# Reordering the front of a fused attention, channel-mix and expert kernel: planner ranks, GpSimd rounding, early weights

## The chip, the cores and the metric

The kernel runs on one core of one Trainium2 chip, in one launch. The metric is the device time of that launch in microseconds (us). Engines are named as in the profile: PE is TensorE, DVE is VectorE, ACT is ScalarE, POOL is GpSimd, SP is SyncE, whose queue issues nearly all DMAs here.

## The reference, cut to what matters

Three stages, each feeding the next: a local and global attention over 4 batches of 8 heads; a channel mix (two mixed inputs, a squared-relu product and a gated product); and a mixture of eight experts, in which every row goes to one expert.

```python
# attention, per batch and head: 512 local rows (window of 32 both ways + 32 global keys), 32 global rows
out_g = sm(scale*q_g @ k_all.T) @ v_all
out_l = sm(concat(scale*q_l @ k_g.T, where(mask, scale*q_l @ k_l.T, -1e9))) @ concat(v_g, v_l)
x = concat(out_g, out_l) per head, heads side by side        # (4, 544, 512)
# channel mix; x_prev is x moved down by one row
xk = mu_k*x + (1-mu_k)*x_prev;  xr = mu_r*x + (1-mu_r)*x_prev
x = sigmoid(xr @ w_r) * (max(xk @ w_k, 0)**2 @ w_v)          # w_k 512x1024, w_r 512x512, w_v 1024x512
# experts: row s goes to e (argmax of x @ w_gate, or the row before's choice)
out[b,s] = p[e] * (max(x @ w1[e], 0) @ w2[e])
```

The inputs w_k, w_r, w_v of the channel mix arrive as 64-bit floats; the kernel reads them as pairs of 32-bit integers.

## The kernel before, in words

**Units.** Attention is cut into 16 units (one batch, two heads); units 0 to 3 make batch 0. A unit is loaded (`load`, L120: q, k and the global rows; `load_v`, L133: ten DMAs for v), transposed into place (`prep`, `prep_g`), and then has two kinds of work. *Items* 0 to 3 are its local rows: `twin` (L178) makes the scores of two items on PE, `item` (L194) does the softmax on DVE (L204), ACT (L208), DVE (L211) and POOL (L214), then PE transposes the weights (L221, tile ptp) and ACT copies them out (tile ph). `gitem` (L284) is item 4, the 32 global rows: scores (L291, tiles sga, sgb), softmax, transposes (L311, tile ptg), copy out (tile ph, by DVE at L114). `values` (L243) multiplies the weights by v: for units 0 to 3 one product for each item as it gets ready (PE tiles av and, for item 4, avg), for units 4 to 15 all five at once. An av product is copied into the channel mix's input xT by ACT (L264). An avg product goes through `turn_g` (L267): ACT scales it (L272, tile og), PE transposes it (L275, tile avt), DVE copies it into xT (L279). A PSUM place "av" of one bank serves av, avg and avt of units 0 to 3, and the place "g" (one) is held from a unit's `gitem` scores until its `turn_g` ends.

**Channel mix.** `weight` (L407) turns one part of w_k (8 parts), w_r (4) or w_v (8) from 64-bit into a rounded 32-bit tile h and a remainder l: a DMA on SP (L417), ACT (L424), three DVE operations (L426, L428, L430), ACT rounds (L432), POOL subtracts (L434). `mix` (L449) makes xk and xr for a group of 256 rows, two of the four 128-row blocks of d_model at a time (blocks 0 and 1 need units 0 and 1, blocks 2 and 3 need units 2 and 3, for batch 0): POOL (L460), DVE (L463), ACT (L465), POOL (L467). PE then multiplies with w_k (tile psk), w_r (psr) and w_v (psv), three products for each (L21, L23, L24). There are nine groups, of which the first lies wholly in batch 0. The experts follow, under an order written out by hand, which the change does not touch.

**What sets the order.** `Sched` (L42) is a planner that runs when the program is built. Each piece of work is a generator of steps; a step names an engine and an assumed duration. At each planned moment, of the steps that are ready it emits the one with the lowest (rank, number in order of addition). SP's DMA issues are an engine ("Q") of the planner too. Ranks: loads -2, w_k parts ahead of the rest PE0=-1.5 (the first N0=3), consts and v loads -1, unit starts and transposes 0, mixes PM=0.5, scores, items, values and `turn_g` 1, other w_k and w_r parts PW=1.5, w_v parts and outputs 2, products of the channel mix 4. The framework beneath may still move an instruction in the emitted order; every engine executes its own list strictly in order.

```python
    for k,i in [("wk",i) for i in range(8)]+...: sched.add(m.weight(k,i),PV if k=="wv" else PE0 if k=="wk" and i<N0 else PW)
```

Of the kernel before, what the change touches and what calls it, by code (L numbers as in the profile page):

```python
# [11 lines left out]
AF=mybir.ActivationFunctionType; ALU=mybir.AluOpType; X=mybir.AxisListType.X  # L12
# [12 lines left out]

N0=3; PE0=-1.5; PC=-1; PW=1.5; PV=2; PM=0.5
NF=4
EV={"kn":"A","qn":"D","g":"D",0:"A",1:"A",2:"A",3:"A"}  # L30
LN=8 ; PL=8
# [8 lines left out]
def op(e,d,need=(),free=(),when=None): return e,d,need,free,when  # L40
def wait(f): return "",0.0,(),(),f
class Sched:  # L42
# [23 lines left out]
    def run(s):  # L66
        while s.L:
            while s.one(): pass
            if not s.L: break
            T=[t for t in [x[3] for x in s.L]+list(s.busy.values())+[t for t,_ in s.left] if t>s.t]  # L70
            assert T, [(x[0],x[2]) for x in s.L]
            s.t=min(T)
            for t,k in s.left:
                if t<=s.t: s.places[k]+=1
            s.left=[y for y in s.left if y[0]>s.t]
# [8 lines left out]
class Attn:  # L84
# [109 lines left out]
    def item(s,sched,u,i,S_,held):  # L194


        nc=s.nc; b,pr=divmod(u,4)
        ks=s.cols(i); w=1 if i in (1,2) else .87
        parts=s.parts(u)
        p=s.pt_.pop(0)  # L200
        mx=s.sb.tile([P,8],F32,tag="mx",name="mx",bufs=5)
        yield op("D",.64*w,(),held)
        for h in range(2):
            i_=nc.vector.tensor_tensor_reduce(out=p[:,h,ks],in0=S_[h],in1=s.mask[:,ks],scale=-0.125,scalar=3e38,op0=ALU.add,op1=ALU.min,accum_out=mx[:,h:h+1])  # L204
        s.free_=[i_.ins.name]
        yield op("A",.2+.93*w)
        for h in range(2):
            nc.scalar.activation(p[:,h,ks],p[:,h,ks],AF.Exp,bias=mx[:,h:h+1],scale=-1.0,accum_out=mx[:,4+h:5+h])  # L208
        nc.scalar.activation(mx[:,4:6],mx[:,4:6],AF.Copy,bias=1e-9)
        yield op("D",.15)  # L210
        nc.vector.reciprocal(mx[:,6:8],mx[:,4:6])  # L211
        yield op("G",.87*w)
        for h in range(2):
            nc.gpsimd.tensor_scalar(out=p[:,h,ks],in0=p[:,h,ks],scalar1=mx[:,6+h:7+h],scalar2=0.0,op0=ALU.mult,op1=ALU.add)  # L214
        yield op("P",.43,("pt","ph"),("p",),when=lambda: u in s.V and s.taken(u))
        s.took[u]+=1
        pt=s.ps.tile([P,2,2,P],F32,tag="pt",name="ptp",bufs=2)
        for c in range(2):

            for h in range(2):  # L220
                nc.tensor.transpose(pt[:,c,h],p[:,h,c*96:c*96+P],s.ident)  # L221
        s.pt_.append(p)
        P_=s.weights()
        yield from s.split(u,EV[i],[P_],pt.rearrange("p c h q -> p c (h q)"),"pt",(.48,.61))
        yield wait(None)
        s.H[u][i]=(P_,s.made)
        if u<NQ: sched.add(s.values(sched,u,(i,),"av"),1)
    def visit(s,after,c=mybir.DependencyClass.NoSync):


# [12 lines left out]
    def values(s,sched,u,which,*place):  # L243


        nc=s.nc; b,pr=divmod(u,4)
        yield op("P",.2+sum(.6 if i==4 else .45 for i in which),place,("ph",)*len(which),when=lambda: u in s.V and all(i in s.H[u] for i in which))
        V=s.V[u]; mm=s.visit([s.H[u][i][-1] for i in which]); rows=[slice(0,HD),slice(HD,P)]
        if 4 in which:
            G,mx=s.H[u][4][:2]  # L250
            og=s.ps.tile([P,512],F32,tag=place[-1],name="avg",bufs=len(place))[:,:HD]
            for c in range(5):
                for h,r in enumerate(rows): mm(og[r],G[:,c*64:(c+1)*64],V[:,min(c,3),c//4,r],start=c==0,stop=c==4)
            sched.add(s.turn_g(u,og,mx,place[-1],len(place)),1)
        s.vdone[u]+=len(which)
        tiles=[i for i in which if i<4]
        if not tiles: return
        o=s.ps.tile([P,512],F32,tag="av",name="av",bufs=1)
        for j,i in enumerate(tiles):
            for c in range(2):  # L260
                for h,r in enumerate(rows): mm(o[r,j*P:(j+1)*P],V[:,i,c,r],s.H[u][i][0][:,c,h*P:(h+1)*P],start=c==0,stop=c==1)
        n=P*len(tiles); c0=1+SG+tiles[0]*P
        yield op("A",.07+.00104*n,(),("av",))
        nc.scalar.activation(s.xT[b][:,pr,c0:c0+n],o[:,:n],AF.Copy)  # L264
        yield wait(None)
        s.odone[u]+=len(tiles)
# [17 lines left out]
    def gitem(s,sched,u):  # L284

        nc=s.nc; b,pr=divmod(u,4); kw,gT=s.T[u]["k"],s.T[u]["g"]
        parts=s.parts(u)
        yield op("P",.75,("s","s","g"))
        a=s.ps.tile([P,512],F32,tag="s",name="sga",bufs=2)[:64]; g=s.ps.tile([P,512],F32,tag="s",name="sgb",bufs=2)[:64,:32]
        for o,k in ((a,kw[:,:,:,32:160]),(g,gT[:,:,64:96])):  # L290
            for m,(x,y_) in enumerate(parts): nc.tensor.matmul(o,gT[:,x,:64],k[:,y_],start=m==0,stop=m==len(parts)-1)  # L291
        s.sdone[u]+=1
        p=s.pg[:64]
        M=s.sb.tile([P,8],F32,tag="mg",name="mxg",bufs=2); mx=M[:64]
        yield op("D",1.1)
        nc.vector.reduce_max(mx[:,0:1],a,axis=X)
        nc.vector.reduce_max(mx[:,1:2],g,axis=X)
        nc.vector.tensor_reduce(out=mx[:,2:3],in_=mx[:,0:2],axis=X,op=ALU.max)
        nc.vector.tensor_scalar(out=mx[:,2:3],in0=mx[:,2:3],scalar1=-0.125,scalar2=None,op0=ALU.mult)
        yield op("A",.92,(),("s","s"))  # L300
        nc.scalar.activation(p[:,32:544],a,AF.Exp,bias=mx[:,2:3],scale=0.125,accum_out=mx[:,4:5])
        s.free_=[nc.scalar.activation(p[:,544:576],g,AF.Exp,bias=mx[:,2:3],scale=0.125,accum_out=mx[:,5:6]).ins.name]
        yield op("D",.28)
        nc.vector.scalar_tensor_tensor(out=mx[:,6:7],in0=mx[:,4:5],scalar=1e-9,in1=mx[:,5:6],op0=ALU.add,op1=ALU.add)
        nc.vector.reciprocal(M[0:32,7:8],mx[0:32,6:7])
        nc.vector.reciprocal(M[96:128,7:8],mx[32:64,6:7])
        yield op("P",.55,("pt","ph"),when=lambda: u in s.V and s.taken(u))
        s.took[u]+=1
        pt=s.ps.tile([P,512],F32,tag="pt",name="ptg",bufs=2)
        for c in range(5):  # L310
            nc.tensor.transpose(pt[:,c*64:c*64+P],s.pg[:,min(c*P,480):min(c*P,480)+P],s.ident)  # L311
        G=s.weights().rearrange("p c q -> p (c q)")[:,:320]
        yield from s.split(u,EV["g"],[G],pt[:,:320],"pt",(.32,.4))
        yield wait(None)
        s.H[u][4]=(G,M,s.made)
        if u<NQ: sched.add(s.values(sched,u,(4,),"av"),1)
    def spare(s,u): return u<4 and u%2==1
    def same(s,u): return [v for v in range(u) if s.spare(v)==s.spare(u)]
    def loads(s,units):
# [3 lines left out]
    def run(s,sched,units,may):  # L323
        for u in units:
            yield wait(lambda: u in s.nat and may(u) and all(s.sdone[v]>=5 for v in s.same(u)))
            s.sdone[u]=s.vdone[u]=s.odone[u]=0; s.H[u]={}; s.took[u]=0
            if s.spare(u): kw,qT,gT=s.kwe,s.qTe,s.gTe
            else:
                dt=F32 if s.early(u) else F32R
                qT=s.sb.tile([P,2,512],dt,tag="qT",name=f"qT{u}",bufs=1); kw=s.sb.tile([P,2,4,224],dt,tag="kw",name=f"kw{u}",bufs=1)  # L330
                gT=s.sb.tile([P,2,96],dt,tag="gT",name=f"gT{u}",bufs=1)
            s.T[u]=dict(k=kw,q=qT,g=gT,n=0,have=False)
            sched.add(s.prep(u,"kn"),0); sched.add(s.prep(u,"qn"),0); sched.add(s.prep_g(u),0)
            yield wait(lambda: s.T[u]["n"]==3)
            for i in (0,2): sched.add(s.twin(sched,u,i),1)
            sched.add(s.gitem(sched,u),1)
            if u>=NQ: sched.add(s.values(sched,u,(4,0,1,2,3),"av","pt"),1)

def band(nc,const):

# [9 lines left out]
class Mix:  # L350
# [56 lines left out]
    def weight(s,k,i):  # L407


        nc=s.nc; place="raw"+"v"*(k=="wv")  # L410
# [11 lines left out]
        h,l=[v(s.W[k+x]) for x in "hl"]  # L422
        m=s.temp("w").rearrange("p (c f) -> p c f",c=c); a=m.bitcast(I32)
# [4 lines left out]
        nc.vector.scalar_tensor_tensor(out=a,in0=hi,scalar=-0x80000000,in1=a,op0=ALU.bitwise_and,op1=ALU.bitwise_or)  # L428
        yield op("D",.6,(),(place,))
        nc.vector.scalar_tensor_tensor(out=a,in0=lo,scalar=29,in1=a,op0=ALU.logical_shift_right,op1=ALU.bitwise_or)  # L430
        yield op("A",.52)
        nc.scalar.activation(h,m,AF.Copy)  # L432
        yield op("G",1.23,(),("r",))
        nc.gpsimd.tensor_sub(l,m,h.bitcast(F32))  # L434
        yield wait(None)
# [284 lines left out]
def phase1(tc,ctx,i,const,y,ident,x,slots,early,place,right):  # L720
# [38 lines left out]
    sched.add(a.run(sched,units,lambda u: u<8 or min(m.mixed)>=(u//4-1)*S),0)  # L759
    for k,i in [("wk",i) for i in range(8)]+[("wr",i) for i in range(4)]+[("wv",i) for i in range(8)]: sched.add(m.weight(k,i),PV if k=="wv" else PE0 if k=="wk" and i<N0 else PW)  # L760
    sched.add(m.mixes(sched,groups),PM)
# [360 lines left out]
```

## Time and profile before

| | |
|---|---|
| median of 3 runs | 742.79 us (742.07 to 744.51) |
| the profiled execution's own time | 741.31 us |
| its span, first to last instruction | 739.6 us |
| PE busy | 682.3 us (92%) |
| DVE, ACT, POOL busy | 444.7, 371.9, 301.4 us |
| mean granted PE clock | 0.961 |

A span is what the profiler's first and last instruction enclose; 1.7 us of the execution lie around it. Rows of a timeline are: start, duration, engine, line, operation, output<-inputs, shape, count; in brackets the idle time of the engine just before it and what ended that. SPq rows are DMA issues on SP's queue. Rows of a table of stretches are: from and to, length, then busy time and count of each engine, the granted PE clock, the DMA share, GB/s. Of a product (L234, L239) the first row stands for all its matmuls.

### The profile page before, as it was taken

The page shows a single profiled execution, that of the slowest core. Times are in us where ns is not written, and L with a number is a line of the kernel's source. Part 1 is how long each engine was busy: PE and PEld are TensorE (multiplying, and loading weights), DVE is VectorE, ACT ScalarE, POOL GpSimd, SP SyncE. Part 2 cuts the span into 40 slices and gives each one's busy share as a digit, 9 for nine tenths or more (in the row PEclk, how much of TensorE's full clock was granted, in tenths as well). Part 3 has the DMA queues.
Part 4 walks back from the last instruction along what each step waited for, and adds up shares of the span by engine and source line. Part 5 has one row for each costly group of instructions (what it writes and reads, how often), then busy time and mean ns, then how long its engine had stood idle before and what let it go on. Part 6 is the DMA issues. An engine that isn't in the chain of part 4 may idle for free. (4 is left out here: it accounts for less than half of the span.)

```text
span 739.6 us, 14192 instructions
## 1 busy us (share of the span) xinstructions
PE 682.3 (92%) x4962; PEld 583.3 (79%) x4962; DVE 444.7 (60%) x1361; ACT 371.9 (50%) x942; POOL 301.4 (41%) x434
## 2 busy tenths in 40 slices
PE   4786969999999999989998999999799999979897
PEld 3564658898888988879987898877689889969785
DVE  6489477857676574774537964778554435324361
ACT  4678576674474663645645432417544325115251
POOL 5457476724443252551423522115725405121431
PEclk9787799999999999999999999999999999999999
DMA  6575154212202211202103200418946607233440
GB/s 156 126 227 167 34 135 136 53 53 55 58 14 58 70 25 52 63 14 70 24 16 131 86 30 15 142 33 292 355 148 188 205 24 235 93 118 129 138 142 22
DMA packets 93184, 76.39 MB, mean 103 GB/s; under 512 B 70350, under 2 KB 74446, under 8 KB 93074
## 3 DMA queue, kind: packets, MB, share of 16 engines
q1 hardware_dynamic: 89618, 64.27, 29.5%
q0 software_dynamic: 3456, 10.75, 4.1%
q8 instruction: 56, 0.92, 0.5%
q14 instruction: 54, 0.44, 0.2%
HBM read 66.08 MB, written 9.44 MB: 102 GB/s over the span
## 5 line engine op out<-in xcount | busy, mean ns | idle before, releaser
L214 POOL TENSOR_SCALAR pl<-pl,mx 128x192 f32<-128x192 f32 (+1 forms) x128 | 64.3, 518 | 97.9 <-DVE mx L211 87.5
L21 PE MATMUL psk<-xs,slot0h 128*128 128x256 f32 x256 | 73.7, 292 | 1.1 <-ACT xs L465 1.1
L24 PE MATMUL psk<-xs,slot0l 128*128 128x256 f32 x256 | 73.4, 287 | 0.0
L23 PE MATMUL psk<-xs,slot0h 128*128 128x256 f32 x256 | 72.9, 285 | 0.0
L208 ACT ACTIVATE pl<-pl,mx 128x192 f32<-128x192 f32 (+1 forms) x128 | 58.6, 460 | 21.4 <-DVE mx L204 17.9
L460 POOL TENSOR_SCALAR xm<-xT,mut 128x256 f32<-128x256 f32 (+6 forms) x96 | 44.5, 479 | 47.4 <-DVE xT L279 15.9
L910 ACT ACTIVATE hh<-ph 128x256 fp32r<-128x256 f32 (+2 forms) x56 | 22.4, 400 | 79.2 <-PE ph L24 52.8
L467 POOL TENSOR_TENSOR xs<-xm,xs 128x512 fp32r<-128x512 f32 (+1 forms) x36 | 45.4, 1272 | 33.1 <-ACT xs L465 33.1
L21 PE MATMUL psv<-slot1h,kh 128*128 128x512 f32 x136 | 54.8, 403 | 0.0
L24 PE MATMUL psv<-slot1h,kl 128*128 128x512 f32 x136 | 54.3, 399 | 0.0
L23 PE MATMUL psv<-slot1l,kh 128*128 128x512 f32 x136 | 54.2, 399 | 0.0
L911 DVE SCALAR_TENSOR_TENSOR hl<-ph,hh 128x256 fp32r<-128x256 f32 (+2 forms) x56 | 24.7, 442 | 47.0 <-ACT hh L910 44.5
L111 ACT ACTIVATE ph<-ptp 128x512 f32<-128x512 f32 x64 | 37.6, 593 | 29.9 <-PE ptp L221 29.8
L21 PEld LDWEIGHTS psk<-xs,slot0h 128*128 128x128 f32 x256 | 48.8, 193 | 1.5 <-ACT xs L465 1.2
L221 PE MATMUL ptp<-ident,pl 128*128 128x128 f32 x256 | 44.8, 301 | 5.3 <-POOL pl L214 4.8
L23 PEld LDWEIGHTS psk<-xs,slot0h 128*128 128x128 f32 x256 | 48.5, 189 | 0.7 <-POOL xs L467 0.2
L24 PEld LDWEIGHTS psk<-xs,slot0l 128*128 128x128 f32 x256 | 48.5, 189 | 0.2
L882 POOL DMA_INDIRECT xs<-y,idx x23 | 26.7, 1163 | 50.5 <-PE pt L889 23.4
L463 DVE SCALAR_TENSOR_TENSOR xm<-xT,mut,xm 128x256 f32<-128x256 f32 (+6 forms) x96 | 39.9, 447 | 7.7 <-POOL xm L460 7.6
L221 PEld LDWEIGHTS ptp<-ident,pl 128*128 128x128 f32 x256 | 32.2, 153 | 13.7 <-POOL pl L214 9.1
L21 PE MATMUL ph<-xh,slot2h 128*128 128x256 f32 (+1 forms) x128 | 37.9, 296 | 2.1 <-issue 2.1
L239 PE MATMUL av<-ph,ve 128*64 128x128 f32 x480 | 37.9, 292 | 0.0
(603 smaller groups left out, 2185.0 us busy)
## 6 DMA issues: line engine op xcount, KB each, us to landing
st<-in_moe_w_dram SPq DMA_DIRECT2D x42, 512.0 KB, 4.2
sw<-in_moe_w_dram SPq DMA_DIRECT2D x22, 512.0 KB, 4.0
y<-r SPq DMA_DIRECT2D x17, 256.0 KB, 2.0
qn<-in_q_l_dram SPq DMA_DIRECT2D x32, 128.0 KB, 2.9
kn<-in_k_l_dram SPq DMA_DIRECT2D x32, 128.0 KB, 2.9
earlyh<-in_moe_w_k_dram SPq DMA_DIRECT2D x8, 512.0 KB, 4.1
raw<-in_moe_w_v_dram SPq DMA_DIRECT2D x8, 512.0 KB, 4.4
ve<-in_v_l_dram SPq DMA_DIRECT2D x32, 96.0 KB, 2.1
```

The source lines that it names most:

```text
L21: i=nc.tensor.matmul(out,wh,xh,start=first,stop=False)
L23: nc.tensor.matmul(out,wh,xl,start=False,stop=False)
L24: return nc.tensor.matmul(out,wl,xh,start=False,stop=last)
L111: s.made=nc.scalar.activation(out[0],x,AF.Copy).ins.name
L208: nc.scalar.activation(p[:,h,ks],p[:,h,ks],AF.Exp,bias=mx[:,h:h+1],scale=-1.0,accum_out=mx[:,4+h:5+h])
L214: nc.gpsimd.tensor_scalar(out=p[:,h,ks],in0=p[:,h,ks],scalar1=mx[:,6+h:7+h],scalar2=0.0,op0=ALU.mult,op1=ALU.add)
L221: nc.tensor.transpose(pt[:,c,h],p[:,h,c*96:c*96+P],s.ident)
L239: with t.high_priority(t.cur_priority-len(first)): i=s.nc.tensor.matmul(*a,**k)
L460: nc.gpsimd.tensor_scalar(out=x[:,u,o:o+k],in0=s.xT[b][:,c,q:q+k],scalar1=m[:,1,c:c+1],scalar2=0.0,op0=ALU.mult,op1=ALU.add)
L463: nc.vector.scalar_tensor_tensor(out=x[:,u,o:o+k],in0=s.xT[b][:,c,1+q:1+q+k],scalar=m[:,0,c:c+1],in1=x[:,u,o:o+k],op0=ALU.mult,op1=ALU.add)
L467: nc.gpsimd.tensor_sub(xl[:,cs,:n],x[:,:,:n],xh[:,cs,:n].bitcast(F32))
L882: s.nc.gpsimd.indirect_dma_start(out=s.xs[i][:,j,:],out_offset=None,in_=s.y,in_offset=IndirectOffsetOnAxis(ap=s.idx[:,ch:ch+1],axis=0))
```

## The change

Three edits, all in the attention and channel-mix stage. N0 goes from 3 to 1: one part of w_k, not three, ranks ahead of unit 0; parts 1 and 2 get PW=1.5 as the others. `values` and `turn_g` are added with rank 0.5 instead of 1. Parts 0 to 3 of w_k are rounded by POOL, not ACT, with a planned 0.6 us.

```diff
-N0=3; PE0=-1.5; PC=-1; PW=1.5; PV=2; PM=0.5
+N0=1; PE0=-1.5; PC=-1; PW=1.5; PV=2; PM=0.5
@@ item
-        if u<NQ: sched.add(s.values(sched,u,(i,),"av"),1)
+        if u<NQ: sched.add(s.values(sched,u,(i,),"av"),0.5)
@@ values
-            sched.add(s.turn_g(u,og,mx,place[-1],len(place)),1)
+            sched.add(s.turn_g(u,og,mx,place[-1],len(place)),0.5)
@@ gitem
-        if u<NQ: sched.add(s.values(sched,u,(4,),"av"),1)
+        if u<NQ: sched.add(s.values(sched,u,(4,),"av"),0.5)
@@ run
-            if u>=NQ: sched.add(s.values(sched,u,(4,0,1,2,3),"av","pt"),1)
+            if u>=NQ: sched.add(s.values(sched,u,(4,0,1,2,3),"av","pt"),0.5)
@@ weight
-        yield op("A",.52)
-        nc.scalar.activation(h,m,AF.Copy)
+        if k=="wk" and i<4:
+            yield op("G",.6)
+            nc.gpsimd.tensor_scalar(out=h,in0=m,scalar1=1.0,scalar2=0.0,op0=ALU.mult,op1=ALU.add)
+        else:
+            yield op("A",.52)
+            nc.scalar.activation(h,m,AF.Copy)
```

## Rows read from the trace of the kernel before

**Rows 1.** The page's busy times.

```profile
PE 682.3 (92%) x4962; PEld 583.3 (79%) x4962; DVE 444.7 (60%) x1361; ACT 371.9 (50%) x942; POOL 301.4 (41%) x434
```

**Rows 2.** Busy time by stretch: PE, PEld, DVE, ACT, POOL, clock, DMA share, GB/s.

```profile
10.00:20.00 10.00, 4.87 (x24) 2.67 (x20) 9.93 (x31) 7.69 (x25) 5.12 (x7) 1.00 0.62 130
...
40.00:76.00 36.00, 26.68 (x179) 18.51 (x177) 32.48 (x87) 28.65 (x88) 26.88 (x32) 0.74 0.62 184
...
94.00:110.00 16.00, 9.33 (x110) 7.51 (x111) 13.46 (x45) 10.97 (x35) 12.56 (x18) 0.89 0.54 141
110.00:480.00 370.00, 363.11 (x2980) 318.24 (x2979) 246.29 (x893) 200.06 (x556) 147.57 (x244) 0.99 0.21 59
```

**Rows 3.** Timeline of PE, 81 to 112 us: products with w_k and stops.

```profile
81.76 0.99 PE L21 MATMUL psk<-xs,slot0h 128*128 128x256 f32 x3
...
101.95 0.55 PE L234 MATMUL s__1314<-kw,qT 64*128 64x224 f32 x1 [3.00 <-DVE mx L204]
...
107.40 0.95 PE L221 MATMUL ptp<-ident,pl 128*128 128x128 f32 x4 [0.53 <-POOL pl L214]
109.79 0.33 PE L275 MATMUL avt<-ident,og 128*128 128x128 f32 x1 [1.44 <-ACT og L272]
109.87 0.36 PE L21 MATMUL psk<-xs,slot0h 128*128 128x256 f32 x1
```

**Rows 4.** Timeline of DVE: copy out of item 4's weights, unit 1; unit 3's last copy.

```profile
49.07 0.49 DVE L114 COPY ph<-ptg 128x320 f32<-128x320 f32 x1
...
102.21 0.38 DVE L279 COPY xT<-avt 64x32 f32<-64x32 f32 x2
```

**Rows 5.** Timeline of PE: item 4's products and their transposes, units 1 and 3.

```profile
64.53 0.27 PE L234 MATMUL avg<-ve,ph 128*64 128x64 f32 x1
...
77.63 0.48 PE L275 MATMUL avt<-ident,og 128*128 128x128 f32 x1
...
95.93 0.24 PE L234 MATMUL avg<-ve,ph 128*64 128x64 f32 x1 [1.07 <-DVE xT L279]
...
98.67 0.27 PE L275 MATMUL avt<-ident,og 128*128 128x128 f32 x1
```

**Rows 6.** Timeline of DVE, 9 to 20 us: weight parts and unit 0's score maxima.

```profile
11.24 0.42 DVE L426 TENSOR_SCALAR w<-w 128x512 int32<-128x512 int32 x1
...
12.17 1.73 DVE L428 SCALAR_TENSOR_TENSOR w<-earlyh,w 128x512 int32<-128x512 int32 x1
...
17.37 0.68 DVE L430 SCALAR_TENSOR_TENSOR w<-earlyh,w 128x512 int32<-128x512 int32 x1
```

**Rows 7.** Timeline of SP: the three early parts; unit 0's last v load.

```profile
5.13 1.53 SPq L417 DMA_DIRECT2D earlyh<-in_moe_w_k_dram  x3
...
20.20 0.43 SPq L143 DMA_DIRECT2D ve<-in_v_g_dram  x1
```

**Rows 8.** The page's DMA issues: v loads, KB each, median us to landing.

```profile
ve<-in_v_l_dram SPq DMA_DIRECT2D x32, 96.0 KB, 2.1
```

**Rows 9.** Timeline of PE: unit 0's first product with v.

```profile
25.10 0.48 PE L234 MATMUL av<-ph,ve 128*64 128x128 f32 x1
```

**Rows 10.** Groups by line and shape, POOL: mixing's scale, two sizes.

```profile
L460 POOL TENSOR_SCALAR xm<-xT,mut 128x224 f32<-128x224 f32 x8 | 3.7, 461 | 0.8 <-DVE last L617 0.8
L460 POOL TENSOR_SCALAR xm<-xT,mut 128x32 f32<-128x32 f32 x8 | 2.3, 293 | 9.6 <-DVE kl L480 9.6
```

**Rows 11.** Timelines, 12 to 62 us: ACT's rounding; POOL and DVE side by side.

```profile
15.45 0.63 ACT L432 ACTIVATE slot0h<-w 128x512 fp32r<-128x512 f32 x1
...
12.07 1.27 POOL L434 TENSOR_TENSOR slot0l<-w,slot0h 128x512 fp32r<-128x512 f32 x1 [3.14 <-ACT slot0h L432]
...
59.28 1.55 POOL L214 TENSOR_SCALAR pl<-pl,mx 128x224 f32<-128x224 f32 x2 [2.04 <-DVE mx L211]
...
59.77 0.74 DVE L428 SCALAR_TENSOR_TENSOR w<-earlyh,w 128x512 int32<-128x512 int32 x1
```

**Rows 12.** Timeline of PE: a product with v that stops it.

```profile
71.10 0.47 PE L234 MATMUL av<-ph,ve 128*64 128x128 f32 x1 [1.43 <-ACT xT L264]
```

## The prediction

> **What bounds the kernel now.** I read the page's busy times first, then busy time by stretch, then the timelines around the stops of PE. PE is busy 682.3 us of a span of 739.6 [rows 1], so over most of the kernel no other engine's time counts. The stretches say where that is not so. From 110 to 480 us PE is busy 363.11 us of 370; from 94 to 110 it is busy 9.33 of 16, from 40 to 76 it is busy 26.68 of 36, and from 10 to 20 it is busy 4.87 of 10 [rows 2]. What the change can win therefore lies ahead of 110 us, and it is won by giving PE the channel mix's products, which it has in plenty, at an earlier time. Shifting attention alone wins only if they come earlier with it.
>
> When do they come? The products with w_k for the first 256 rows begin at 81.76 and break off: only two of the four blocks of their input are there. They go on at 109.87, and from there PE is full. In between PE stops, among others, for 3.00, 0.53 and 1.44 us, behind attention's softmax and ACT [rows 3]. The missing blocks need units 2 and 3, of which the last piece of xT is written at 102.21 [rows 4]. So batch 0's last value product is what holds the end, by way of the idle stretch from 94 to 110.
>
> Why is it so late? Item 4 of unit 1 shows it. Its weights are copied out by 49.07 + 0.49 = 49.56 [rows 4], but its product with v runs at 64.53, 15.0 us later, and the transpose that belongs to that product at 77.63, 13.1 us later. For unit 3, where little stands between, the same two steps are 95.93 and 98.67: 2.7 us, which is what they cost by themselves [rows 5]. The rest of unit 1's waits is rank: product and transpose have rank 1 and a late number, so the planner put the next units' scores and softmax ahead. The place "g" is held all that time, and no later unit's global scores may start; one more unit, unit 2, has the same pattern.
>
> **The change, part by part.** *Products with v at rank 0.5.* Nothing is added or removed: the same instructions stand earlier in PE's, ACT's and DVE's lists, ahead of the next unit's scores. What is gained is bounded below by nothing (if batch 0's end does not move) and above by all idle time of PE from 94 to 110: 16 - 9.33 = 6.67 us [rows 2]. For the stops after 98.94 (101.95 - 3.00) to be filled, the second half of the w_k products has to come by then, so 109.87 - 98.94 = 10.9 us earlier [rows 3]. Unit 1's two waits alone hold 15.0 + 13.1 - 2.7 = 25.4 us beyond their own work [rows 4, 5]; not all can go, for the engines in between work through lists with DVE busy 32.48 of 36 us [rows 2], but half of it is enough. I take those three stops, 3.00 + 0.53 + 1.44 = 4.97 us, as filled, nearer to the upper end. What is late next is the softmax of batch 1, which then stands behind the values; PE has products with w_k to cover that. Units 4 to 15 gain next to nothing: their values were already added ahead of their items.
>
> *One part ahead of unit 0.* Off DVE's path in front of unit 0's score maxima come two parts at 0.42 + 0.68 + 0.68 = 1.78 us, and a stall: the operation at 12.17 took 1.73 where its like takes 0.68. That is 3.56 + 1.05 = 4.61 us [rows 6], in a stretch where DVE is busy 9.93 of 10 us [rows 2]. On SP two of three issues go, 2/3 of 1.53 = 1.02 us [rows 7], and the constants, unit 1's loads and v all move up by as much. That puts a limit on the gain: the last v load of unit 0 is issued at 20.20 [rows 7] and lands 2.1 later [rows 8], at 22.3, while the first product with v starts at 25.10 [rows 9]. So 2.80 us are free, and with SP's 1.02 the product can move 3.8 us, unless SP also takes v ahead of unit 1's loads. Ends: 1.0 (SP alone) and 4.6 (DVE alone); I take 3.8, DVE's gain up to v's arrival.
>
> The two parts come back later: each has its DMA issue, its ACT scaling, DVE operations and GpSimd subtract. SP, ACT and GpSimd have room for them; on DVE they cost 3.56 us, and between 40 and 76 us it is 90% busy [rows 2]. Ends: 0, if they fit where DVE rests, and 3.6. I take 3.6, as the stretch with most of the conversions is the full one. Front gain and return nearly cancel: -3.8 + 3.6 = -0.2.
>
> *Four roundings on GpSimd.* Off ACT go four times 0.63 us [rows 11]. GpSimd has no row of this size; one-input operations there take 293 ns for 32 columns and 461 for 224 [rows 10], 0.875 ns a column, so for 512 columns 461 + 288 x 0.875 = 713 ns: an estimate, with the 1.27 us of the two-input subtract [rows 11] as its upper end. As the subtract follows on the same engine, the chain of a part is as long as before, and what covers the work is GpSimd's free time, 9 us between 40 and 76 [rows 2]. I cost it at nothing. Its ends are a gain of 3 x 0.63 = 1.9 us, if ACT set the pace for the three parts behind the first, and a loss of 4 x 0.71 = 2.8, if GpSimd holds up DVE each time. For the loss: against a subtract DVE's operation took 1.73 instead of 0.68 [rows 6, 11]. Against it: beside one-input operations of GpSimd it took 0.74, and the two of GpSimd took 1.55 [rows 11], so there GpSimd was the one to wait. The Trainium skill (SBUF — State Buffer, Who interferes with whom) says that a VectorE operation with two SBUF inputs and a GpSimd operation that reads SBUF lock each other out for a whole instruction, the one issued second waiting. The trace agrees at 12.17 and leaves open at 59.77 who comes second; by the rule alone the sum would be that of the third rival.
>
> **Sum.** -0.2 - 5.0 = -5.2 us. The profiled execution took 741.31 us, its span plus 1.7 around it, and is 1.48 below the median; against it the change gives 736.1, against the median of 742.79 it gives 737.6, which is my forecast. With every bound at its good end it is -4.6 - 6.67 - 1.9 = -13.2, or 729.6; with the front at its bad end (-1.0 + 3.6) and the stops filled, -2.4, or 740.4: this case's own range.
>
> **Rivals.** *The ranks do not move batch 0's end*, because PE's order is made again beneath the planner, or because softmax and not rank held unit 3. For it: PE's stop of 3.00 us waits for DVE's maxima [rows 3]. Against it: 15 us between finished weights and their product. Then the front is left: -0.2, or 742.6.
>
> *Values stop PE* (the other side). PE works in order; a product placed right behind its transposes waits there for ACT's copy, with the next unit's scores behind it, and DVE and ACT behind those. One such stop, for ACT's copy out of the place av, is 1.43 us [rows 12]. With one more unfilled in each of the four units and batch 0's end no earlier, 4 x 1.43 - 0.2 = +5.5, or 748.3. It decides from two such stops: 2 x 1.43 - 0.2 is over 2.2. Against it: in the stretches ahead of 76 us PE idles anyway, so most of these stops would take the place of others.
>
> *GpSimd holds DVE.* Four roundings block 0.71 us each, and the subtracts of the two returned parts meet a DVE operation each, 2 x 1.05 [rows 6]: -5.2 + 2.8 + 2.1 = -0.3, or 742.5. Against it: the row at 59.77.
>
> **How the numbers follow.** About 0.3%, 2.2 us, can be told from no change: faster is below 740.6, slower above 745.0. The forecast's case has 0.63, the first rival 0.13, the third 0.07, the second 0.17. So faster 0.63, same 0.20, slower 0.17. The range reaches from 731.0, near the good end of the likeliest case, to 745.5, over both rivals without effect; the second rival stays outside for the most part.
>
> **What would show it.** Right: unit 0's first product with v near 21 us instead of 25.10; item 4's product of unit 1 within some 5 us of its weights' copy; the second half of the w_k products before 99; PE busy over 14 of 16 us from 94 to 110; a rounding on GpSimd of about 0.7 us; 110 to 480 as full as before. Wrong: products with w_k that still go on at about 110; stops of PE in front of av products that add up to several us; operations of L428 or L430 at 1.4 us beside a rounding; or the front won and an equal loss behind 110, where PE is idle 6.89 us of 370 [rows 2] and a new order can open other stops.

## The result, and the profile after

The changed kernel takes 734.1 us (730.21 to 734.79, 4 runs) against 742.43 (742.03 to 744.51): ratio 0.9881, interval 0.9845 to 0.9918. That is 8.3 us less; forecast were 5.2. The profiled execution took 733.44 us, its span is 731.7.

Busy time by stretch after, with the columns of [rows 2]:

```profile
10.00:20.00 10.00, 5.10 (x25) 3.59 (x23) 6.04 (x32) 5.93 (x25) 5.33 (x11) 0.77 0.47 105
20.00:40.00 20.00, 14.85 (x124) 10.56 (x125) 13.63 (x50) 13.64 (x45) 10.50 (x18) 0.94 0.72 203
40.00:76.00 36.00, 25.00 (x219) 17.14 (x217) 27.42 (x77) 27.17 (x87) 27.84 (x35) 0.92 0.65 184
76.00:94.00 18.00, 15.00 (x134) 11.79 (x134) 14.33 (x49) 13.85 (x44) 12.34 (x20) 0.88 0.20 45
94.00:110.00 16.00, 15.15 (x163) 14.13 (x162) 11.58 (x41) 13.39 (x41) 10.10 (x15) 1.00 0.51 141
110.00:480.00 370.00, 361.09 (x2949) 314.09 (x2948) 249.79 (x921) 195.02 (x545) 140.07 (x237) 1.00 0.20 58
```

From 94 to 110 us PE is now busy 15.15 of 16 us instead of 9.33, as the products with w_k are there. PE's timeline after shows when they begin and when their second half goes on:

```profile
72.64 0.62 PE L21 MATMUL psk<-xs,slot0h 128*128 128x256 f32 x3 [1.81 <-ACT xs L469]
...
98.04 0.62 PE L21 MATMUL psk<-xs,slot0h 128*128 128x256 f32 x3
99.39 0.38 PE L23 MATMUL psk<-xs,slot0h 128*128 128x256 f32 x1 [0.73 <-POOL xs L471]
```

They go on at 98.04, where before they did at 109.87 [rows 3]. But in this execution PE's idle time is not what fell. I cut both executions where the first product with w_r starts and where the last product with w_v ends. The stretches of the kernel before, then of the kernel after, with the same columns (front, channel mix, experts):

```profile
0.00:121.80 121.80, 88.58 (x677) 67.84 (x678) 84.90 (x270) 81.95 (x253) 72.84 (x133) 0.83 0.52 140
121.80:481.10 359.30, 352.82 (x2889) 307.94 (x2888) 236.61 (x868) 191.62 (x534) 140.78 (x234) 0.99 0.20 56
481.10:739.60 258.50, 240.90 (x1400) 207.56 (x1398) 123.16 (x224) 98.34 (x155) 87.78 (x67) 0.98 0.46 152
```

```profile
0.00:110.60 110.60, 78.94 (x673) 60.60 (x674) 77.27 (x261) 77.38 (x247) 73.46 (x134) 0.92 0.55 147
110.60:471.20 360.60, 352.34 (x2893) 307.32 (x2891) 241.94 (x877) 192.56 (x538) 140.07 (x237) 1.00 0.21 58
471.20:731.70 260.50, 241.51 (x1401) 207.39 (x1398) 122.99 (x224) 98.05 (x155) 87.01 (x67) 0.98 0.45 151
```

The front is 11.2 us shorter; channel mix and experts give back 1.3 and 2.0. In the front PE is idle 121.80 - 88.58 = 33.2 us before and 31.7 after, while its busy time falls by 9.6 us with about as many instructions: the granted clock rose from 0.83 to 0.92. The granted clock stands at one of two levels, 1.2 or 2.4 GHz, so 2 x 0.17 x 121.8 = 41 us of the front ran at 1.2 GHz before, and 2 x 0.08 x 110.6 = 18 us after. What was idle from 94 to 110 came back ahead of it: from 40 to 94 PE was idle for 10.5 us before (9.3 of them in [rows 2], the rest in the row below) and for 14.0 after.

```profile
76.00:94.00 18.00, 16.83 (x136) 12.50 (x134) 6.53 (x33) 10.75 (x37) 6.64 (x12) 0.75 0.11 33
```

So in this execution the shorter front is mostly less busy time: PE does about the same work at the higher level. The runs below show that this split is not the same in every kernel with the new ranks.

### The profile page after: what moved, and what is told of

It is laid out like the page before. It is cut to its first block, busy times and chain, and to the rows that moved or that the text cites. A ratio compares the mean times of both kernels' runs of the same rounds, so it can differ in the third digit from the quotient of the medians.

```text
span 731.7 us, 14196 instructions
## 1 busy us (share of the span) xinstructions
PE 672.8 (92%) x4962; PEld 575.3 (79%) x4962; DVE 442.2 (60%) x1361; ACT 368.0 (50%) x938; POOL 300.5 (41%) x438
## 5 line engine op out<-in xcount | busy, mean ns | idle before, releaser
L24 PE MATMUL psk<-xs,slot0l 128*128 128x256 f32 x256 | 71.7, 282 | 0.0
L208 ACT ACTIVATE pl<-pl,mx 128x224 f32<-128x224 f32 (+1 forms) x128 | 58.7, 460 | 23.7 <-DVE mx L204 21.1
L464 POOL TENSOR_SCALAR xm<-xT,mut 128x256 f32<-128x256 f32 (+6 forms) x96 | 43.0, 466 | 43.3 <-DVE xT L279 14.7
L467 DVE SCALAR_TENSOR_TENSOR xm<-xT,mut,xm 128x256 f32<-128x256 f32 (+6 forms) x96 | 41.7, 471 | 13.1 <-POOL xm L464 13.0
L221 PE MATMUL ptp<-ident,pl 128*128 128x128 f32 x256 | 42.0, 288 | 5.9 <-ACT ph L111 2.1
L23 PE MATMUL ph<-xl,slot2h 128*128 128x256 f32 (+1 forms) x128 | 37.1, 290 | 0.0
```

The costliest lines, as they stand in the source:

```text
L23: nc.tensor.matmul(out,wh,xl,start=False,stop=False)
L24: return nc.tensor.matmul(out,wl,xh,start=False,stop=last)
L464: nc.gpsimd.tensor_scalar(out=x[:,u,o:o+k],in0=s.xT[b][:,c,q:q+k],scalar1=m[:,1,c:c+1],scalar2=0.0,op0=ALU.mult,op1=ALU.add)
L467: nc.vector.scalar_tensor_tensor(out=x[:,u,o:o+k],in0=s.xT[b][:,c,1+q:1+q+k],scalar=m[:,0,c:c+1],in1=x[:,u,o:o+k],op0=ALU.mult,op1=ALU.add)
```

## The experiments

Theories: that the *ranks* carry the gain; that the *front* does (two parts out of unit 0's way, SP's queue moving up); that the *clock* is the cause, whatever edit raises it. Runs with each subset of the three edits, all against the kernel before on the same chip (742.4 to 744.4 us in the different sets); lengths of the stages come from one profiled execution of each kernel, while executions of the kernel before on one chip lie between 739.95 and 748.40 us, so a few us between two stage lengths can be chance:

| edits | median us | ratio, interval | front, mix, experts us |
|---|---|---|---|
| ranks | 739.71 | 0.9945, 0.9926 to 0.9965 | 110.7, 367.6, 259.6 |
| N0=1 | 750.15 | 1.0082, 1.0050 to 1.0113 | 116.0, 369.4, 263.5 |
| GpSimd | 739.90 | 0.9943, 0.9919 to 0.9967 | 120.4, 364.6, 252.8 |
| ranks, GpSimd | 733.82 | 0.9854, 0.9822 to 0.9885 | 108.9, 364.2, 261.5 |
| ranks, N0=1 | 739.78 | 0.9935, 0.9901 to 0.9969 | 115.0, 362.2, 262.1 |
| N0=1, GpSimd | 743.73 | 0.9988, 0.9966 to 1.0010 | 118.3, 363.0, 259.9 |
| all | 734.10 | 0.9881, 0.9845 to 0.9918 | 110.6, 360.6, 260.5 |

**The ranks alone.**

```diff
-... values and turn_g added with rank 1
+... values and turn_g added with rank 0.5     (N0=3, roundings on ACT)
```

> Only the four ranks go from 1 to 0.5. Theory of ranks: this edit carries the gain, 734 to 738 us (before 742.4), the second half of the w_k products resumes before 99 us instead of 109.87, and PE is busy over 14 of the 16 us from 94 to 110. Theory of the front (the two parts moved out from ahead of unit 0 carry it): 741 to 744, products resume near 110. Theory of the clock (the gain is PE time at the lower granted level, 24.3 us extra before and 11.9 after, while idle time stays near 57 us): the time follows the mean granted clock over the first 110 us whichever edit it is; a mean clock of the kernel near 0.975 gives 734 to 737, one near 0.96 gives 741 to 744.

Measured 739.71. The second half of the w_k products and the stretch from 94 to 110 are as the theory of ranks has them:

```profile
97.48 0.51 PE L21 MATMUL psk<-xs,slot0h 128*128 128x256 f32 x2
```

```profile
94.00:110.00 16.00, 16.00 (x171) 14.86 (x170) 11.40 (x41) 13.17 (x41) 7.92 (x14) 0.98 0.30 66
```

The whole front gain, 11.1 us, is there with this edit by itself; 8.3 us of it are given back in the channel mix (367.6 against 359.3) and 1.1 in the experts, so the time stays above the 734 to 738 expected.

**N0 alone.**

```diff
-N0=3
+N0=1
```

> Only N0 goes from 3 to 1. Theory of ranks: front gain and the two parts' return cancel, 741 to 744 us, w_k products resume within 3 us of 109.87. Theory of the front: 735 to 738, as the whole of SP's queue behind the first unit moves up (v of unit 0 issued from 8.36 instead of 15.88). Theory of the clock: as the mean granted clock goes, 0.975 for 734 to 737 and 0.96 for 741 to 744.

Measured 750.15, which no theory had. The w_k products go on at 104.14 and the front is 5.8 us shorter, but mix and experts are 10 and 5 us longer. As the cause of the gain, the theory of the front falls.

**GpSimd's roundings alone.**

```diff
+        if k=="wk" and i<4: yield op("G",.6); nc.gpsimd.tensor_scalar(out=h,in0=m,...)
+        else: yield op("A",.52); nc.scalar.activation(h,m,AF.Copy)
```

> Only the four roundings go to GpSimd. Theory of ranks and theory of the front: 741 to 744 us. If ACT set the pace of the early parts: 739 to 741. If GpSimd's rounding holds DVE: 743 to 746, with operations of DVE lines 428 and 430 above 1.3 us beside a rounding.

Measured 739.90, within the range of the theory on ACT's pace, and the w_k products go on at 104.51. But front and mix together are 485.0 us against 481.1 before: all the gain is in the experts' stage, 252.8 against 258.5, where nothing is rounded by this edit. The run with padding below shows what that is worth.

**Without N0's edit.**

```diff
-N0=1
+N0=3        (ranks 0.5, roundings on GpSimd)
```

> The changed kernel with N0 back at 3 (ranks and roundings changed). Theory of ranks: 734 to 738 us. Theory of the front: 741 to 744. If the edits only work together: near 742 here and near 742 in the run with the ranks alone.

Measured 733.82, the same as all three within the intervals. N0's edit adds nothing.

**Without GpSimd's roundings, and without the ranks.**

```diff
-        if k=="wk" and i<4: ... GpSimd ...          (no_gp: N0=1, ranks 0.5)
-... rank 0.5
+... rank 1                                         (no_v: N0=1, GpSimd)
```

> The changed kernel with the four roundings back on ACT (N0=1 and ranks 0.5). Theory of pairs (ranks and roundings make the gain together: ranks bring the w_k products forward, but with the roundings on ACT the later weight parts come late and PE stops for 8 us between 110 and 200, as with the ranks alone): 738 to 742 us. Theory that ranks and N0 carry it and the rounding is hidden: 733 to 736.

> The changed kernel with the ranks back at 1 (N0=1, roundings on GpSimd). Theory of ranks: 740 to 748 us, second half of the w_k products no earlier than 102 us. Theory of sums of single effects (-3.1 of the roundings and +7 of N0): 746 to 748.

739.78 and 743.73. The second goes with the theory of ranks: the w_k products go on at 104.70 there. The first has the time of the theory of pairs, but not its mechanism: PE is idle for 6.6 us from 110 to 200, not 8, and the w_k products go on at 103.78, where N0 alone had them at 104.14. So beside N0=1, with the roundings on ACT, the ranks hardly move batch 0's end. By ratios the ranks take off 0.55% alone, 1.5% beside N0 (0.9935/1.0082), 0.9% beside GpSimd (0.9854/0.9943), 1.1% beside both (0.9881/0.9988): always a gain. N0 costs 0.8%, gains 0.1%, costs 0.45% and 0.3% in the same way: never a gain that can be told.

**PE kept busy in the front**, on the kernel before:

```diff
-                nc.tensor.transpose(pt[:,c,h],p[:,h,c*96:c*96+P],s.ident)
+                for again in range(3 if u<NQ else 1): nc.tensor.transpose(pt[:,c,h],p[:,h,c*96:c*96+P],s.ident)
```

> The kernel before, with every transpose of item weights in units 0 to 3 made three times over (128 transposes more, same output). Theory of the clock (PE's slow level from 67 to 85 us is what costs time, and it comes from PE standing still): the lower level shrinks below 40 us in all and the time falls to 736 to 742 although PE does more. Theory of order (the clock only follows from attention's waits, which stay): 743 to 752, the lower level still near 59 us or the stretch to the first w_r product no shorter than 121 us.

Measured 747.67, ratio 1.0045 (1.0014 to 1.0076). Its front:

```profile
0.00:125.30 125.30, 96.27 (x805) 78.68 (x806) 82.73 (x269) 82.30 (x253) 74.40 (x133) 0.89 0.50 136
```

The clock rises from 0.83 to 0.89 (28 us at the lower level instead of 41), yet the front grows by 3.5 us. In this run the clock rose with a busier PE, and batch 0's end came forward by no more than 3.4 us (products go on at 106.45). The run also added PE work, but two kernels of the table compare fronts at nearly one clock. First with ranks and GpSimd, then with N0=1 and GpSimd:

```profile
0.00:108.90 108.90, 84.26 (x672) 64.38 (x673) 76.17 (x252) 74.49 (x237) 66.57 (x126) 0.86 0.52 140
```

```profile
0.00:118.30 118.30, 88.00 (x678) 67.44 (x679) 83.99 (x266) 79.16 (x249) 76.58 (x137) 0.87 0.54 144
```

Both have about 30 us at the lower level, and the front with the ranks is 9.4 us shorter, though the other one has N0's edit, which by itself takes 5.8 us off it. Of its 12.9 us against the kernel before, 8.6 are idle time (33.2 to 24.6) and 4.3 busy time; with the ranks alone it is 4.7 (33.2 to 28.5) and 6.4. So the clock by itself does not make the front shorter: the order moves batch 0's end, and how the gain splits into less idle time and a higher clock differs from kernel to kernel.

**Are late w_v parts what gives the front gain back?**

```diff
-PV=2
+PV=1.5      (ranks alone changed otherwise)
```

> The kernel with the ranks alone changed, and the w_v parts' rank (and that of the rest under PV) at 1.5 instead of 2. Theory of late weights (the ranks' front gain of 11 us is given back between 110 and 200 because w_v parts are converted last, up to 155 us): last w_v remainder before 145 us, PE idle from 110 to 200 at most 5 us instead of 8.4, time 734 to 738. If something else gives it back: 738 to 743 and idle as before.

Measured 739.18. The last w_v remainder comes at 157, not before 145, and PE's idle time from 110 to 200 is 90 - 80.61 = 9.4 us:

```profile
110.00:200.00 90.00, 80.61 (x653) 66.73 (x652) 69.65 (x218) 55.49 (x157) 49.06 (x76) 0.98 0.30 80
```

The edit did not do what it was for: the rank of these parts is not what holds them. The theory was not tested by it.

**Padding.** On the kernel before, with no other edit:

```diff
+    pad=ps.tile([P,512],F32,tag="av",name="pad",bufs=1)
+    for _ in range(24): nc.tensor.transpose(pad[:1,:1],ident[:1,:1],ident[:1,:1])
     sched.run()
```

> The kernel before with 24 one-element transposes on PE ahead of everything, while PE waits for its first data: nothing else is changed. It shows what a change without an effect of its own does. If the length of the expert stage (252.7 to 263.5 us in the runs so far, with the same instructions in it) hangs on where PE's instructions lie, the stage leaves 256 to 261 us here and the time moves by more than 2 us either way. If it hangs on the front's order, the stage stays within 1.5 us of 258.5 and the time within 742 to 745.

Measured 735.81, ratio 0.9880 (0.9841 to 0.9920): as much as the whole change. PE's timeline begins with the padding, in time that was idle:

```profile
1.62 0.73 PE L766 MATMUL pad<-ident 1*1 1x1 f32 x24 [1.62 <-POOL ident masks.py:199]
5.92 1.09 PE L160 MATMUL ptq<-ident,kn 128*128 128x128 f32 x4 [3.57 <-DMA kn<-in_k_l_dram]
```

All 4962 other PE instructions stand in the same order, and so do those of the other engines. Its front is 1.1 us shorter, its mix 0.5 us, its experts' stage 4.4 us. Stage and time are as the theory of position has them:

```profile
479.50:733.60 254.10, 239.51 (x1400) 206.00 (x1398) 123.29 (x224) 98.22 (x155) 88.08 (x67) 0.99 0.47 154
```

PE's timeline of the kernel before, in the experts, has the stop that is missing with the padding:

```profile
661.99 0.45 PE L21 MATMUL ph<-xh,slot1h 128*128 128x352 f32 x1 [3.97 <-issue]
```

"issue" says that PE waits for nothing that the profile shows. Behind this stop the granted clock is down (0.83 from 660 to 670 us), and products of this shape take 0.49 us instead of the 0.32 with the padding. The list of who PE waited for in the experts has 6.0 and 2.0 us of "issue" before, 5.0 with the padding, 4.0 with GpSimd's roundings alone (line, total, times, longest):

```profile
PE ph L21 <- issue: 6.0, 2, 4.0
PE po L24 <- issue: 2.0, 1, 2.0
```

```profile
PE ph L21 <- issue: 5.0, 2, 3.6
```

```profile
PE ph L21 <- issue: 4.0, 3, 3.0
```

The other ten runs, the changed kernel and the kernel before have 7.6 to 10.6 us of it in all and experts' stages of 258.5 to 263.5 us, where padding and GpSimd alone have 254.1 and 252.8. And the long stop has a fixed place. Counted over all of PE's records in the trace (products, weight loads, and the semaphore, register and branch instructions that the rows leave out), exactly 9373 stand ahead of it in the kernel before and in ten of the others, though the product it delays differs:

```profile
654.26 0.45 PE L21 MATMUL ph<-xh,slot1h 128*128 128x352 f32 x1 [3.11 <-issue]
```

```profile
661.96 0.45 PE L23 MATMUL ph<-xl,slot1h 128*128 128x352 f32 x1 [3.81 <-issue]
```

These are the changed kernel and the ranks alone. The run with repeated transposes, with 256 records more, has it behind 9629. The block of products that begins behind 9372 records in the kernel before begins behind 9421 with the padding and 9379 with GpSimd alone, past that place, and there is no such stop.

So a shift of PE's instructions that does nothing moves this kernel's time by over 1%. In the profiled executions 4.4 of the 6.0 us are in the experts' stage, and 3.0 of these are stops that hang on no data. What causes the stop at that place of PE's list was not tried.

The table has to be read with this in mind: differences of a per cent between its totals can be position, and the gain of GpSimd alone is about what the missing stop is worth. What stands apart from it is the front, which lies ahead of the experts: with the ranks it is 11.1 us shorter alone, 11.5 beside GpSimd, 7.7 beside both and 1.0 beside N0, where N0 by itself had already taken 5.8; the padding moved it by 1.1. With N0=3, the five kernels that have the ranks (three of them are runs outside the table) have fronts of 108.9 to 112.4 us, and the four without, the padding among them, 120.4 to 125.3. So the ranks' place and sign rest on the front; how much of each total is theirs is not known to better than about 1%.

**Rank 0.6.**

```diff
-... rank 0.5
+... rank 0.6      (all else as changed)
```

> The changed kernel with rank 0.6 instead of 0.5 for the values and their transposes: still ahead of scores (1), but behind the mixes (0.5). Theory of ranks (what counts is being ahead of scores): 732 to 737 us, w_k products resume before 101 us. If being level with the mixes carries it: 739 to 744.

734.21, ratio 0.9866 (0.9828 to 0.9904); products go on at 98.74. By this run standing ahead of the scores is what counts, not being level with the mixes.

**The planned engine without the engine, and more roundings.**

```diff
             yield op("G",.6)
-            nc.gpsimd.tensor_scalar(out=h,in0=m,...)
+            nc.scalar.activation(h,m,AF.Copy)            (vg_on_act: ranks 0.5, N0=3)
-        if k=="wk" and i<4:
+        if k=="wk":                                      (vg8: ranks 0.5, N0=3)
```

> Ranks 0.5 and N0=3, with the four roundings planned as GpSimd's 0.6 us but executed by ACT. It tells the planned order from the engine. If ACT's relief is what the roundings bring (739.7 with the ranks alone, 733.8 with ranks and roundings): 738 to 741 us. If it is the other order that the planner finds: 732 to 736.

> Ranks 0.5, N0=3, and all eight w_k roundings on GpSimd instead of four. If ACT's relief brings the gain of the roundings, four more take ACT another 2.5 us off and the time falls to 729 to 733 us; if GpSimd, busy 20.85 of 36 us from 40 to 76 with four, is then late with its subtracts: 734 to 738.

740.45, ratio 0.9946 (0.9924 to 0.9969), and 738.81, ratio 0.9925 (0.9897 to 0.9954). With the work left to ACT the gain of the roundings is gone, though the planner reckoned with GpSimd: by the totals it is the engine, not the plan. The stop at the fixed place does not tell them apart (2.83 us with ACT, 3.88 with GpSimd), though 0.9% is as much as position has made elsewhere. The w_v remainders show a difference by their first and last start, with the roundings on ACT and then on GpSimd:

```profile
L438 POOL TENSOR_TENSOR slot1l<-w,slot1h x8: 1264/1364/1757, 112.6 to 155.8; 128x512 fp32r<-128x512 f32 x8
```

```profile
L438 POOL TENSOR_TENSOR slot1l<-w,slot1h x8: 1278/1286/1459, 107.8 to 144.9; 128x512 fp32r<-128x512 f32 x8
```

They end 11 us earlier with ACT relieved, and the mix is 3 us shorter (364.2 against 367.1). The two profiled executions differ by 2.2 us (738.55 and 736.33), the medians by 6.6, so the profiles show only part of the gain. Eight roundings do not go further: the last remainder starts at 136.6, 8 us earlier still, but the front is 112.1 and the mix 364.9. So earlier remainders are not shown to be what carries the gain. Four are worth more than none and than eight, and the experiments do not show why eight lose.

## Why the prediction was right, point by point

**What bounds.** Right. Batch 0's end held the channel mix, and the four ranks alone move it: 97.48 and a full stretch from 94 to 110. The bound of 10.9 us for filling the three stops was met, 109.87 - 98.04 = 11.8.

**The total.** Right within its range, and in part by luck. The front gave 11.2 us where the sum had 5.2, and 3.3 went back behind it, which the sum had at nothing and only the signs of being wrong spoke of: from 110 to 480 PE is idle for 8.9 us instead of 6.89. Two wrong terms of N0 cancelled, and the roundings gained where the sum had nothing. And padding that does no work took off as much as the whole change, so the total alone would not have shown that the mechanism was right; the front does.

**The ranks, -5.0 us.** Right in sign and place; off in size. The runs give 0.55% to 1.5%, 4 to 11 us. The step took the gain as idle time filled, 4.97 us. In the front idle time fell by 1.5 us with all three edits, 4.7 with the ranks alone and 8.6 with ranks and GpSimd, and PE's busy time, at a higher mean clock, by 9.6, 6.4 and 4.3. The prediction had the clock's rows in hand, 0.74 from 40 to 76 us [rows 2], and gave the clock no term: that is what was left out. Of the way there, one step was too bold. Item 4's product of unit 1 was to run within 5 us of its weights' copy:

```profile
41.35 0.48 DVE L114 COPY ph<-ptg 128x320 f32<-128x320 f32 x1
```

```profile
52.09 0.27 PE L234 MATMUL avg<-ve,ph 128*64 128x64 f32 x1
...
57.82 0.28 PE L275 MATMUL avt<-ident,og 128*128 128x128 f32 x1
```

It runs 10.3 us after the copy, and its transpose 5.7 later; before it was 15.0 and 13.1 [rows 4, 5]. The rank shortened the waits to about half, as the sum had asked, not to their own work.

**N0, -3.8 and +3.6 us.** The sum, about nothing, agrees with the pairs beside the ranks (0.1% gained, 0.3% lost). The edit cost 0.45% beside GpSimd, where the stop that GpSimd alone lacks is back (3.22 us), and 0.8% alone, which stays unexplained. Both terms are wrong. The first product with v was to start near 21 us. SP's queue and PE after:

```profile
8.36 0.38 SPq L139 DMA_DIRECT2D ve<-in_v_l_dram  x1
...
13.20 1.22 SPq L126 DMA_DIRECT2D qn<-in_q_l_dram  x2
14.46 1.31 SPq L126 DMA_DIRECT2D kn<-in_k_l_dram  x2
...
27.21 2.26 SPq L417 DMA_DIRECT2D earlyh<-in_moe_w_k_dram  x4
```

```profile
18.13 1.09 PE L160 MATMUL ptq<-ident,kn 128*128 128x128 f32 x4 [4.44 <-DMA kn<-in_k_l_dram]
...
21.79 0.84 PE L221 MATMUL ptp<-ident,pl 128*128 128x128 f32 x4
...
24.65 0.27 PE L234 MATMUL avg<-ve,ph 128*64 128x64 f32 x1
```

SP took the constants and v ahead of unit 1's keys (issued at 14.46, before the change at 7.02). PE, in order, stood 4.44 us for those keys with unit 0's transposes behind them, so DVE's earlier end of unit 0 (6.04 us busy from 10 to 20 instead of 9.93) reached PE as 24.65 instead of 25.10 [rows 9]. The prediction named that SP might take v first, and did not ask what PE would then wait for. The return of the two parts cost DVE nothing either: SP issued four parts at 27.21, DVE worked on them between 31.7 and 44.4, and from 40 to 76 it is busy 27.42 us instead of 32.48.

**The roundings, 0.** A rounding takes 0.616 us (estimated 0.71), and the cover held: GpSimd is busy 27.84 of 36 us from 40 to 76. What was mis-sized is the gain: 0.9% beside the ranks (739.71 to 733.82), 0.5% beside ranks and N0 (0.9881/0.9935, where the front goes from 115.0 to 110.6), about 6 and 4 us where the upper end was 1.9. With them the later parts end 10 us sooner than with the ranks alone, but what carries the gain, and how much of it is position, stays open.

**The rivals.** *Ranks do not move batch 0's end*: no, by the runs. *Values stop PE*: such stops are there, but no more of them than before. In front of av products PE stops for 0.87, 0.73, 0.40 and 0.35 us in the front, 2.4 in all, where it was 0.20, 0.26, 1.73 and 1.43 before; the longest one:

```profile
39.86 0.32 PE L234 MATMUL av<-ph,ve 128*64 128x128 f32 x1 [0.87 <-ACT xT L264]
```

*GpSimd holds DVE*: the rows of POOL and then of DVE after:

```profile
38.91 0.61 POOL L433 TENSOR_SCALAR slot0h<-w 128x512 fp32r<-128x512 f32 x1
39.60 1.27 POOL L438 TENSOR_TENSOR slot0l<-w,slot0h 128x512 fp32r<-128x512 f32 x1
41.52 0.62 POOL L433 TENSOR_SCALAR slot0h<-w 128x512 fp32r<-128x512 f32 x1 [0.64 <-DVE w L430]
42.22 1.58 POOL L438 TENSOR_TENSOR slot0l<-w,slot0h 128x512 fp32r<-128x512 f32 x1
```

```profile
39.82 1.60 DVE L430 SCALAR_TENSOR_TENSOR w<-earlyh,w 128x512 int32<-128x512 int32 x1
41.35 0.48 DVE L114 COPY ph<-ptg 128x320 f32<-128x320 f32 x1
41.75 0.92 DVE L428 SCALAR_TENSOR_TENSOR w<-earlyh,w 128x512 int32<-128x512 int32 x1
42.71 1.64 DVE L430 SCALAR_TENSOR_TENSOR w<-earlyh,w 128x512 int32<-128x512 int32 x1
```

Beside the subtracts DVE's operation takes 1.60 and 1.64 us instead of 0.68 [rows 6], beside a rounding (41.52) 0.92. The lock of which the Trainium skill speaks (SBUF — State Buffer, Who interferes with whom), between a VectorE operation with two SBUF inputs and a GpSimd operation that reads SBUF, shows in all three: GpSimd had started first, and DVE ends 0.55, 0.55 and 0.53 us after GpSimd's operation does (40.87, 43.80 and 42.14). The rounding cost DVE only 0.24 us because DVE came when 0.39 us of it were left. With ranks and GpSimd (N0=3) DVE came first, and the rounding took 0.99 us instead of 0.62:

```profile
15.55 0.99 POOL L433 TENSOR_SCALAR slot0h<-w 128x512 fp32r<-128x512 f32 x1 [1.56 <-DVE w L430]
```

```profile
15.39 0.68 DVE L428 SCALAR_TENSOR_TENSOR w<-earlyh,w 128x512 int32<-128x512 int32 x1
```

So the rival's mechanism is there, but not at its price: of the four roundings after, one delayed an operation of L428 by 0.24 us and one an operation of L426 (34.16) by 0.3, and DVE, busy 27.42 of 36 us from 40 to 76, had room for that and for the two subtracts, 0.92 and 0.96.

## What to carry to other kernels

Where a planner or a list fixes the order, look for finished data that waits for its consumer: the gap from a copy to the product that reads it was the row that found the gain. Split a bundle of edits into all its subsets before crediting one; here one of three did nothing or harm. And before crediting a gain of 1% to any edit, run one with padding that does no work, and cut the execution into stages: a gain in a stage whose work the edit leaves alone may come from the position of instructions.

## What had not been expected of the hardware

24 one-element transposes in 0.73 us of idle time at the start took 1.2% off. With them a stop of 3.97 us is gone some 650 us later; it waits for nothing the profile shows, and stands behind 9373 records of PE in eleven kernels, whichever product is there. And PE's busy time fell by 9.6 us in the front with 673 instead of 677 products, with 18 us instead of 41 at the lower clock level. The lock between VectorE and GpSimd shows for a one-input rounding as for a subtract: in the cases above, the 512-column VectorE operation or rounding that came second ended 0.47 to 0.55 us after the other.
